# Row 0's first loads as float32 through SyncE, row 7's loads earlier, late stores in parts, and a new order of the work

## The chip, the cores and the metric

The kernel runs on one core of a Trainium2 chip. TensorE (PE) multiplies matrices into PSUM; VectorE (DVE), ScalarE (ACT) and GpSimd (POOL) do the elementwise work; SyncE (SP) issues transfers. Sixteen DMA engines move data between the chip's main memory and the on-chip SBUF. Each compute engine works through its own list of instructions in order and waits for others by semaphores. The metric is the device time of one execution in microseconds; the kernel before has a median of 102.69 us over three runs (101.49 to 103.97).

## The reference

Windowed attention is followed by a gated low-rank mixture of experts, with 8 batch rows, 8 heads, 576 positions and a head size of 64. Four heads see the last 32 positions, four see every fourth of the last 128. Everything is float32.

```python
scores = scale * np.matmul(q, k.transpose(0, 1, 3, 2))
scores = np.where(masks, scores, -1e9)
attn = np.exp(scores - scores.max(-1, keepdims=True))
x = np.matmul(attn / attn.sum(-1, keepdims=True), v)      # -> (4608, 512)
logits = x @ w_gate                                       # 8 experts
topk = np.argpartition(-logits, 2, axis=1)[:, :2]         # the two largest
w = softmax(logits at topk)
out = x + sum over the two experts of w * ((x @ A[e]) @ B[e])   # rank 16
```

## The kernel before, in words

The work is cut into 8 rows (`r`, one for each batch entry) and two head groups (`g`; 0 and 1). Each step is an operation with a name, and the name carries its row and group. For one row:

- **Loads.** `L...` on GpSimd's queue brings q, k and v and casts float32 to bfloat16 on the way, into one of four slots of SBUF. Row 0 has four of them (`Lk00`: q and k of group 0; `Lk01`; `Lv00`, `Lv01`: v), row 1 two (`L10` and `L11`), rows 2 to 6 one each, row 7 eight (`Lq7gh` with q and k, `Lv7gh` with v, for each group and each half of the partitions). A row from 4 on reuses a slot, and its load waits for the scores and values of the row four before.
- **Scores.** `S0rg` and `S1rg` (two parts of five and four segments) first multiply a mask into PSUM and then q and k on top; `E0rg` and `E1rg` on ScalarE take the exponential (line 341).
- **Values.** `Vrg` multiplies by v, which carries a column of ones for the sum; `Rrg` (line 377) takes the reciprocal and `Nrg` (line 380) divides, both on VectorE, into the float32 tile `x`. `Brg` (line 387) on GpSimd casts to bfloat16.
- **Adapters.** `Trg` and `Ur` transpose on TensorE (lines 404 and 428), `Crg`, `Cdr`, `Cpr` copy back on ScalarE; `Z0r` and `Z1r` multiply by the first weights, `Y..` copies; a chain of small VectorE steps finds the two largest logits; `gzr` (line 489, GpSimd) gates, `Gr` transposes, `gcr` and `gnr` copy; `Drn` multiplies by the second weights and `Arn` adds to `x`.
- **Store.** `Or` on SyncE's queue writes `x` out (lines 582 and 586): rows 0 to 5 whole, rows 6 and 7 in two halves by group. Each store waits for its row's sums and for a list `late` of row 7's loads: the four `Lq7..` and two of the `Lv7..`. Stores with a two-letter name also wait for the store before the last, so that at most two are under way.

Ahead of all this come constants (`con`, a SyncE load; `cc`, `cd` on ScalarE), the adapter weights (`awf` by ScalarE's queue, line 242, cast by `awc` on VectorE; `btf` by SyncE's queue, line 243, cast by `btc` on ScalarE), cleared tiles (`pz`, `xz`, `vz`), and scratch matmuls on a zero tile that keep TensorE occupied: `warm` (five) and `F0`, `F1`, `F2` (two, two, one), each one issued as two passes. All TensorE operations but transposes are issued through a helper at line 211.

What sets the order is a text, `PLAN`: a list of operation names, with the PSUM bank behind an `@`. Operations are issued in that order, each one to its engine's list, so each engine's order is that of the text. Loads stand in GpSimd's list between its casts and gates, stores in SyncE's. In the old text the first scratch matmuls stand ahead of row 0, `F0` behind its first scores, `F1` behind `V01`, and `F2` behind `T00`. Row 0's first scores wait for `Lk00`.

Of the kernel before, what the change touches and what calls it, by code (L numbers as in the profile page):

```python
# [6 lines left out]
FP = mybir.dt.float32  # L7
# [157 lines left out]
def program(nc=None, qkv=None, aw=None, bt=None, con=None, out=None):  # L165
# [10 lines left out]
    XB = [sb(f"xb{i}", [128, 2, XG], BF) for i in range(2)]  # L176
    XT = [sb(f"xt{i}", [128, 4, 640], BF) for i in range(2)]
# [46 lines left out]
    scratch("warm", 5, ["wz"], 1.05)  # L224
    for i, (_, n) in enumerate(FILL):
# [6 lines left out]
    add("cc0", "ACT", ("el", SEG), lambda: [nc.scalar.copy(CON[:, 0:SEG], ONE[:, 0:SEG])], ["con"])  # L232
    add("cc1", "ACT", ("el", 5 * SEG), lambda: [nc.scalar.copy(
        CON[:, 3 * SEG :].rearrange("p (s n) -> p s n", s=5), ONE[:, 0:SEG].unsqueeze(1).to_broadcast([128, 5, SEG]))], ["con"])
# [7 lines left out]
    add("awf", "ACT", ("dma", 128, 2176), lambda: [nc.scalar.dma_start(out=AWF[:, :], in_=aw)])  # L242
    add("btf", "SP", ("dma", 128, 2048), lambda: [nc.sync.dma_start(out=BTF[:, :], in_=bt)])
# [12 lines left out]
    for i in range(SLOTS):  # L256
        for a in range(2):
            if i < 2:
                add(f"vz{i}{a}", "DVE", ("zero", 1170), lambda i=i, a=a: [nc.vector.memset(zeros(i, a), 0)])
            else:  # L260
                add(f"vz{i}{a}", "ACT", ("el", 1170), lambda i=i, a=a: [nc.scalar.copy(
                    zeros(i, a).bitcast(FP), WARM[half(a), 0:2].bitcast(FP).to_broadcast([64, 1170]))], ["wz"])
# [17 lines left out]
    def loads(r):  # L280
        if r == 0:
            for g in range(2):
                a = load(f"Lk{r}{g}", r, [(h, QK_AT[h][g], QK) for h in range(2)], [])
                b = load(f"Lv{r}{g}", r, [(h, V_AT[h][g], VB) for h in range(2)], [])
                qk_ready[r, g], v_ready[r, g] = [a], [b]
# [18 lines left out]
    def attention(r, g):  # L304
        t = IN[r % SLOTS] if nc is not None else None
        i = (2 * r + g) % NP
# [4 lines left out]
        for part, (b0, nb) in enumerate(((0, 5), (5, 4))):  # L311
            k = Bank(2)

            def scores(b0=b0, nb=nb, k=k):
# [13 lines left out]
                for j in range(nb):  # L328
                    n = SEG if b0 + j < NB - 1 else 64
                    for pr, a, c in tiles:  # L330
                        q = QK_AT[a][g] + pr * S + 64 * (b0 + j)
                        done.append(mm(
                            PS[half(c), k.at + pr, j * SEG : j * SEG + n],
                            t[half(a), q + 2 * S : q + 2 * S + 64], t[half(a), q : q + n], False, j == nb - 1,
# [3 lines left out]
            s = add(f"S{part}{tag}", "PE", ("s", nb, 4 + 4 * nb), scores, qk_ready[r, g] + ["con"] + cuts * g, k)  # L338
# [20 lines left out]
        def values():  # L359
# [24 lines left out]
            [va, rc], k)  # L384
        cut = 512 if (r, g) == (B - 1, 1) else XG
        free = [f"T{r - 2}{g}", f"U{r - 2}"] if r > 1 else []
# [186 lines left out]
    for r in range(B):  # L573
# [4 lines left out]
        adapters(r)  # L578
    for r in range(B):
        more = [f"A{r}3"] if r in SHARED else []  # L580
        if r < B - 2:
            add(f"O{r}", "SP", ("dma", 128, 9216), lambda r=r: [nc.sync.dma_start(out=out[r], in_=X[r][:, :])],
                [f"A{r}{n}" for n in range(3)] + more + late)
        else:
            for g in range(2):
                add(f"O{r}{g}", "SP", ("dma", 128, 4608), lambda r=r, g=g: [nc.sync.dma_start(
                    out=out[r][:, XG * g : XG * g + XG], in_=X[r][:, XG * g : XG * g + XG])],
                    [f"A{r}{g}", f"A{r}2"] + more * (1 - g) + late)
# [12 lines left out]
Z01@7 Y01 S021@5 m01 top1 E021 S020@3 S120@1 s121 tt1 th1 g21 gz1 E020  # L601
V21@5 E120 G1@3 R21 gn1 V20@0 gc1 N21 D12@3 R20 D11@6 vz31 A12 N20
S030@4 B20 E030 D10@0 S130@2 E130 S131@4 E131 B21 A11 A10 S031@6 E031 L5
U2@0 T21@5 V30@1 Cd2 T20@4 R30 C21 N30 B30 V31@5 Cp2 R31 N31 L6
C20 Z12@0 Y12 Z02@1 Y02 m02 m12 s122 S141@2 E141 S140@5 E140 T30@7 S041@1
tt2 th2 E041 B31 U3@0 S040@5 C30 V41@1 Cd3 Cp3 top2 g22 gz2 G2@0
E040 gn2 gc2 R41 N41 T31@4 V40@5 D22@3 R40 A22 N40 C31 Z03@0 Z13@2
Y03 m03 Y13 S150@3 m13 s123 D20@0 E150 S151@6 E151 S051@4 D21@2 top3 tt3
th3 B41 B40 A20 T41@7 E051 g23 A21 gz3 U4@1 T40@0 C41 Lq700
Lq711 Lq701 S050@2 Lv710 Cp4 V51@5 R51 N51 Cd4 G3@1 E050 V50@2 R50 N50  # L610
C40 gn3 Z14@0 gc3 B51 Y14 Z04@5 Y04 S060@0 B50 D30@6 E060 S160@4 Lq710
E160 Lv711 Lv701 S161@2 E161 D32@1 Lv700 A30 T50@0 S061@6 A32 C50 m14 m04
top4 V60@1 s124 tt4 T51@4 th4 U5@0 E061 V61@5 O0 R60 N60 O1 S170@2
Cp5 g24 C51 Cd5 Z05@1 E170 R61 Z15@4 Y05 Y15 gz4 N61 G4@0 B60
gn4 D31@6 m05 gc4 B61 S070@2 E070 S171@4 A31 m15 T60@0 top5 E171 s125
tt5 th5 g25 S071@6 O2 O3 V70@1 R70 T61@4 E071 C60 V71@5 U6@0 N70
# [65 lines left out]
```

## Time and profile before

| what | before |
|---|---|
| median of three runs | 102.69 us (101.49 to 103.97) |
| span of the profiled execution | 99.7 us (its whole time isn't given apart from the span) |
| PE, ACT, DVE, POOL busy | 82%, 72%, 61%, 50% |
| casting loads on GpSimd's queue (q0) | 14.23 MB written, 71.2% of 16 engines |
| SyncE's transfers (q1) | 9.77 MB, 23.8% |
| read from and written to main memory | 29.07 MB and 9.44 MB, 386 GB/s over the span |

The span runs from the first to the last instruction of one profiled execution; the runs' times include what lies around it. Queue q0 counts the bytes as written in bfloat16; it reads twice as many. The page cuts the span in 40 slices, with the busy share of each in tenths, and ends with the chain of work that ended last. A stretch of a trace gives, in this order, its length, the busy time of PE, weight loads, DVE, ACT and POOL, the granted TensorE clock, the DMA share and GB/s. A line of the timeline gives start, duration, engine, source line, operation and, in brackets, how long the engine had stood idle and what released it.

### The profile page before, as it was taken

Reading aid. Unit: us, or ns where it says so; the run is one execution under the profiler, and the core shown is the slowest. Engines: PE = TensorE matmul, PEld = TensorE weight load, DVE = VectorE, ACT = ScalarE, POOL = GpSimd, SP = SyncE. Lnnn points to the kernel's source line nnn. Section 1 sums busy time; section 2 is a strip of 40 time slices with the busy share of each in tenths; the row PEclk is TensorE's granted clock in tenths of the full one; section 3 lists DMA queues with packets and bytes.
Section 4 is the critical chain, followed back from the end, with each engine's and each line's share of the span. In section 5 each row is a group of like instructions: output and inputs, shape, how many; then the busy total and the mean of one; then the engine's idle time right before and its main releaser. Section 6 shows DMA issues by size and latency. Waiting matters only on the chain.

```text
span 99.7 us, 3591 instructions
## 1 busy us (share of the span) xinstructions
PE 81.6 (82%) x1585; PEld 59.4 (60%) x1585; DVE 61.3 (61%) x138; ACT 71.7 (72%) x123; POOL 50.1 (50%) x68
## 2 busy tenths in 40 slices
PE   5994989997886879779988997999999999867300
PEld 3331476466653757458856875787788888745100
DVE  5800008854589237945954599197598499989700
ACT  5830771398798897598599588979979999956300
POOL 5999001860453050480872445848448328666810
PEclk9999999999999999999999999999999999999965
DMA  2999999998999989999898999897899999869994
GB/s 51 290 194 183 200 218 208 219 262 182 234 212 196 245 190 252 193 206 235 184 257 184 226 218 198 123 203 157 133 241 408 422 410 422 358 288 414 414 412 183
DMA packets 4447, 24.50 MB, mean 246 GB/s; under 512 B 720, under 2 KB 848, under 8 KB 3024
## 3 DMA queue, kind: packets, MB, share of 16 engines
q0 software_dynamic: 2560, 14.23, 71.2%
q1 hardware_dynamic: 1728, 9.77, 23.8%
q10 hardware_dynamic: 144, 0.28, 0.8%
q8 instruction: 12, 0.20, 0.7%
q14 instruction: 3, 0.02, 0.1%
HBM read 29.07 MB, written 9.44 MB: 386 GB/s over the span
## 4 chain that ended last, share of the span: by engine, by line
PE 53%; ACT 18%; DMA 8%; DVE 7%; POOL 6%; issue 4%; POOLq 0%
PE ps L211 46%; ACT p L341 8%; DMA in<-in_qkv_dram 8%; PE ps L404 4%; DVE x L380 3%; POOL gz L489 3%; PE ps L494 3%; ACT xt L414 2%; POOL x L549 1%; DVE x L541 1%; POOL xb L387 1%; ACT xt L417 1%; DVE tt L479 1%; ACT th L481 1%; ACT zs L462 1%
## 5 line engine op out<-in xcount | busy, mean ns | idle before, releaser
L341 ACT ACTIVATE p<-ps 128x960 bf16<-128x960 f32 (+1 forms) x32 | 27.6, 892 | 7.9 <-PE ps L211 7.6
L387 POOL CAST xb<-x 128x1152 bf16<-128x1152 f32 (+1 forms) x16 | 17.6, 1113 | 23.4 <-DVE x L380 23.4
L211 PE MATMUL ps<-in,p 128*64 128x130 bf16 (+1 forms) x416 | 21.4, 221 | 1.4 <-ACT p L341 1.0
L380 DVE TENSOR_TENSOR x<-ps,rec 128x1152 f32<-128x1152 f32 x16 | 21.7, 1356 | 0.5
L211 PEld LDWEIGHTS ps<-in,p 128*64 128x64 bf16 (+1 forms) x416 | 17.1, 104 | 4.6 <-ACT p L341 1.6
L377 DVE RECIPROCAL rec<-ps 128x18 f32<-128x18 f32 x16 | 4.3, 270 | 22.7 <-PE ps L211 22.5
L541 DVE TENSOR_TENSOR x<-x,ps 128x1024 f32<-128x1024 f32 (+1 forms) x16 | 17.3, 1113 | 1.2 <-PE ps L211 1.2
L271 POOL DMA_DIRECT2D in<-in_qkv_dram x32 | 16.9, 564 | 0.8 <-POOLq L665 0.8
L489 POOL TENSOR_TENSOR gz<-zs,g 128x640 bf16<-128x640 f32 x7 | 8.9, 1274 | 16.1 <-DVE g L484 16.1
L211 PE MATMUL ps<-warm 128*128 128x512 f32 x20 | 12.2, 751 | 1.2 <-DVE warm L215 1.2
L211 PE MATMUL ps<-aw,xt 128*128 128x136 bf16 x160 | 11.2, 223 | 1.0 <-ACT xt L420 0.4
L211 PEld LDWEIGHTS ps<-in 64*64 64x64 bf16 x576 | 10.7, 106 | 2.1
L211 PE MATMUL ps<-in 64*64 64x96 bf16 (+1 forms) x576 | 11.5, 200 | 0.0
L414 ACT COPY xt<-ps 128x1024 bf16<-128x1024 bf16 x8 | 8.1, 1016 | 4.1 <-PE ps L404 4.0
L211 PEld LDWEIGHTS ps<-aw,xt 128*128 128x128 bf16 x160 | 9.6, 98 | 1.9 <-ACT xt L420 0.7
L404 PE MATMUL ps<-one,xb 128*128 128x128 bf16 x128 | 9.6, 220 | 0.7 <-issue 0.5
L404 PEld LDWEIGHTS ps<-one,xb 128*128 128x128 bf16 x128 | 7.6, 97 | 2.2 <-POOL xb L387 0.9
L462 ACT COPY zs<-ps 128x408 f32<-128x408 f32 (+1 forms) x14 | 6.1, 443 | 3.4 <-PE ps L211 3.3
L211 PE MATMUL ps<-bt,gc 128*128 128x256 bf16 (+1 forms) x48 | 6.7, 256 | 1.5 <-ACT gc L510 0.7
L211 PEld LDWEIGHTS ps<-warm 128*128 128x128 f32 x20 | 4.4, 239 | 5.8 <-issue 4.5
L211 PE MATMUL ps<-bt,gn 128*128 128x256 bf16 (+1 forms) x48 | 6.9, 264 | 1.1 <-DVE x L380 0.5
L211 PE MATMUL ps<-one 64*64 64x384 bf16 (+1 forms) x64 | 5.9, 361 | 2.4 <-DMA in<-in_qkv_dram 1.8
(53 smaller groups left out, 91.9 us busy)
## 6 DMA issues: line engine op xcount, KB each, us to landing
in<-in_qkv_dram POOLq DMA_DIRECT2D x10, 868.5 KB, 17.7
out_dram<-x SPq DMA_DIRECT2D x6, 1152.0 KB, 5.8
in<-in_qkv_dram POOLq DMA_DIRECT2D x10, 288.0 KB, 6.8
out_dram<-x SPq DMA_DIRECT2D x4, 576.0 KB, 3.5
in<-in_qkv_dram POOLq DMA_DIRECT2D x10, 146.2 KB, 8.2
in<-in_qkv_dram POOLq DMA_DIRECT2D x2, 434.2 KB, 14.5
awf<-in_aw_dram ACTq DMA_DIRECT2D x1, 272.0 KB, 2.8
btf<-in_bt_dram SPq DMA_DIRECT2D x1, 256.0 KB, 3.1
```

The lines of the kernel that those rows point to most:

```text
L211: return nc.tensor.matmul(o, lhsT=lhsT, rhs=rhs, start=start, stop=stop, skip_group_check=True)
L271: nc.gpsimd.dma_start(out=IN[r % SLOTS][half(a), at : at + n], in_=qkv[r, a, :, at - 2 * VB * a : at - 2 * VB * a + n],)
L341: return [nc.scalar.activation(p[:, :, :].rearrange("p h (s c) -> p h s c", c=PER)[:, :, b0 : b0 + nb, 0:SEG], PS[:, k.at : k.at + 2, 0 : ...
L377: rc = add(f"R{tag}", "DVE", ("el", 60), lambda: [nc.vector.reciprocal(rec[:, :].rearrange("p (b i) -> p b i", b=3), PS[:, k.at : k.at + 3 ...
L380: nm = add(f"N{tag}", "DVE", ("el", XG), lambda: [nc.vector.tensor_tensor(X[r][:, XG * g : XG * g + XG].rearrange("p (b i n) -> p b i n", ...
L387: add(f"B{tag}", "POOL", ("el", cut), lambda: [nc.gpsimd.tensor_copy(XB[r % 2][:, g, 0:cut], X[r][:, XG * g : XG * g + cut])], [nm] + free)
L404: nc.tensor.transpose(tp[j][:, 128 * u : 128 * u + 128], xb[:, g, 256 * u + 128 * j : 256 * u + 128 * j + 128], ident())
L414: return [nc.scalar.copy(xt[:, 0:2, 0:S].rearrange("p j (c i) -> p j c i", c=C)[:, :, :, 0:128], tp.rearrange("p j (i c) -> p j c i", c=C))]
L462: zc.append(add(f"Y{st}{r}", "ACT", ("el", len(us) * ZW), lambda us=us, k=k: [nc.scalar.copy(zs[:, us[0] : us[-1] + 1].rearrange("p u n -> ...
L489: return [en.tensor_tensor(GZ[i][:, us[0] : us[0] + n, :].rearrange("p u (e r) -> p u e r", e=E), zv()[:, us[0] : us[0] + n, 0:ER].rearran ...
L494: return [nc.tensor.transpose(bank(k, n).bitcast(BF)[:, 128 * u : 128 * u + 128], GZ[i][:, u], ident()) for n in range(k.size) for u in us ...
L541: return [nc.vector.tensor_tensor(v, v, PS[:, k.at : k.at + nk].rearrange("p b n -> p (b n)"), ALU.add)]
```

## The change

Five things change together.

1. Row 0's q and k of group 0 no longer come by `Lk00`. SyncE fetches them as float32 into the tile of `x` that row 5 uses much later (`H0`, columns 0 to 351 of each of the four segments, and `H1`, 352 to 575; two transfers each). VectorE casts the q half, ScalarE the k half (`h00`, `h01`, `h10`, `h11`) into the `xb` tile of row 1 (`FIRST`), and row 0's first scores read them there. Scores of part 0 wait for the casts of `H0`; those of part 1 for all four. The cast of row 1 into that tile waits for these scores.
2. The weights `awf` and `btf` wait for `H1`. In the new text `awf` stands behind row 0's exponentials in ScalarE's list.
3. Row 7's loads stand elsewhere in the text: `Lq701` and `Lq700` behind row 2's transposes, `Lv711`, `Lq710` and `Lv701` around row 5's scores, the last three behind row 6's first steps. The list `late` has only `Lq700` and `Lq701`.
4. Rows 4 to 6 are stored in halves, row 7 in four parts, the last of them a quarter of the row's main part.
5. The order text is new throughout. Scratch matmuls `warm` are three instead of five, and all of `F0`, `F1`, `F2` stand ahead of row 0's first scores.

```diff
+    FIRST = XB[1][:, :, :].rearrange("p g n -> p (g n)") if nc is not None else None
...
-    scratch("warm", 5, ["wz"], 1.05)
+    scratch("warm", 3, ["wz"], 1.05)
...
-    add("awf", "ACT", ("dma", 128, 2176), lambda: [nc.scalar.dma_start(out=AWF[:, :], in_=aw)])
-    add("btf", "SP", ("dma", 128, 2048), lambda: [nc.sync.dma_start(out=BTF[:, :], in_=bt)])
+    early, parts = X[5], ((0, 352), (352, S))
+    for n, (c0, c1) in enumerate(parts):
+        def fetch(c0=c0, c1=c1):
+            return [nc.sync.dma_start(
+                out=early[half(a), :].rearrange("p (s n) -> p s n", s=4)[:, :, c0:c1],
+                in_=qkv[0, a, :, QK_AT[a][0] - 2 * VB * a : QK_AT[a][0] - 2 * VB * a + QK].rearrange("p (s n) -> p s n", s=4)[:, :, c0:c1],
+            ) for a in range(2)]
+
+        add(f"H{n}", "SP", ("dma", 128, 16 * (c1 - c0), 2), fetch)
+        for x, (eng, s0) in enumerate((("DVE", 0), ("ACT", 2))):
+            def cast(c0=c0, c1=c1, s0=s0, eng=eng):
+                o, i = [t[:, 576 * s0 : 576 * s0 + 1152].rearrange("p (s n) -> p s n", s=2)[:, :, c0:c1] for t in (FIRST, early)]
+                return [nc.vector.tensor_copy(o, i) if eng == "DVE" else nc.scalar.copy(o, i)]
+
+            add(f"h{n}{x}", eng, ("el", 2 * (c1 - c0)), cast, [f"H{n}"] + ["tab"] * x)
+    add("awf", "ACT", ("dma", 128, 2176), lambda: [nc.scalar.dma_start(out=AWF[:, :], in_=aw)], ["H1"])
+    add("btf", "SP", ("dma", 128, 2048), lambda: [nc.sync.dma_start(out=BTF[:, :], in_=bt)], ["H1"])
...
-                late.extend(qk_ready[r, g] + v_ready[r, g] * g)
+                late.extend(qk_ready[r, g] * (1 - g))
...
-                        q = QK_AT[a][g] + pr * S + 64 * (b0 + j)
+                        q = (0 if first else QK_AT[a][g]) + pr * S + 64 * (b0 + j)
+                        w = FIRST if first else t
...
+            ready = [f"h{n}{x}" for n in range(part + 1) for x in range(2)] if first else qk_ready[r, g]
...
+        free = [f"T{r - 2}{g}", f"U{r - 2}"] if r > 1 else ["S000", "S100"] if r == 1 else []
...
+        if r < 4:
+            store(f"O{r}", r, [(0, 2 * XG)], [f"A{r}{n}" for n in range(3)])
+        elif r < B - 1:
+            for g in range(2):
+                store(f"O{r}{g}", r, [(XG * g, XG * g + XG)], [f"A{r}{g}", f"A{r}2"] + more * (1 - g))
+        else:
+            store(f"O{r}0", r, [(0, 512)], [f"A{r}0"])
+            store(f"O{r}1", r, [(XG, XG + 1024)], [f"A{r}1"])
+            store(f"O{r}2", r, [(1024, XG), (XG + 1024, 2 * XG)], [f"A{r}2"])
+            store(f"O{r}3", r, [(512, 1024)], more)
...
-con awf btf wz tab cc0 pz1 pz0 Lk00 cc1 vz21 vz00 Lk01 xz0
-vz01 warm@7 cd3 Lv00 xz1 cd2 S100@1 pz3 cd0 Lv01 L11 S000@5 E000 F0@4
-btc cd1 L10 E100 S001@6 S101@4 V00@1 E101 awc L2 E001 V01@5 R00 F1@0
-N00 B00 T00@4 C00 R01 F2@3 N01 B01 U0@6 Cp0 Cd0 T01@7 C01
-L3 L4 S111@2 S011@0 Z00@7 E011 Y00 Z10@0 vz10 vz11 Y10 pz2 m00 m10
-s120 E111 S110@6 S010@4 top0 tt0 th0 g20 E110 gz0 E010 V11@0 R11 N11
-G0@7 V10@3 B11 R10 gc0 N10 gn0 D02@7 D00@0 B10 A02 T11@6 vz20 D01@2
-vz30 C11 U1@7 Cd1 Cp1 T10@4 A00 C10 S121@0 E121 A01 Z11@2 Y11 m11
...
+wz warm@3 F2@1 tab con cc1 cd3 pz2 F0@3 vz00 vz10 pz3 H0 H1
+F1@0 pz0 vz11 h10 Lv00 cd2 Lk01 Lv01 L11 L10 vz20 L2 h00 L3
+pz1 cc0 h11 h01 S100@0 vz31 cd1 cd0 E100 S000@3 E000 vz01 V00@2 R00
+N00 S001@0 S101@6 E101 E001 V01@3 R01 B00 N01 awf awc xz0 T00@6 C00
+S011@4 S111@0 E011 E111 B01 U0@3 T01@7 Cd0 V11@4 C01 L4 R11 Cp0 Z00@2
+btf Y00 Z10@3 N11 Y10 S010@4 E010 m10 S110@0 m00 s120 top0 B11 tt0
+th0 g20 gz0 E110 V10@3 G0@7 R10 vz21 xz1 T11@6 N10 btc B10 gc0
+D01@0 S121@3 gn0 C11 E121 A01 L5 S021@5 E021 S120@1 S020@3 T10@0 V21@5 R21
+N21 E020 E120 V20@1 R20 C10 U1@4 Cp1 D02@5 N20 Cd1 Z01@6 D00@2 vz30
...
```

More of the change, by code (lines that the diff above doesn't have):

```diff
@@ L305, in attention @@
         t = IN[r % SLOTS] if nc is not None else None
+        first = r == g == 0
         i = (2 * r + g) % NP
@@ L578, in program, with store, emit @@
         adapters(r)
+    def store(name, r, cuts, deps):
+        def emit():
+            return [nc.sync.dma_start(out=out[r][:, c0:c1], in_=X[r][:, c0:c1]) for c0, c1 in cuts]
+        add(name, "SP", ("dma", 128, 4 * sum(c1 - c0 for c0, c1 in cuts), len(cuts)), emit, deps + late)
     for r in range(B):
         more = [f"A{r}3"] if r in SHARED else []
-        if r < B - 2:
-            add(f"O{r}", "SP", ("dma", 128, 9216), lambda r=r: [nc.sync.dma_start(out=out[r], in_=X[r][:, :])],
-                [f"A{r}{n}" for n in range(3)] + more + late)
-        else:
[L585 to L588, printed above, removed]
+        if r < 4:
[3 more added lines that the diff above has]
+                store(f"O{r}{g}", r, [(XG * g, XG * g + XG)], [f"A{r}{g}", f"A{r}2"] + more * (1 - g))
+        else:
+            store(f"O{r}0", r, [(0, 512)], [f"A{r}0"])
+            store(f"O{r}1", r, [(XG, XG + 1024)], [f"A{r}1"])
+            store(f"O{r}2", r, [(1024, XG), (XG + 1024, 2 * XG)], [f"A{r}2"])
+            store(f"O{r}3", r, [(512, 1024)], more)
@@ L601 @@
[L601 to L616, printed above, removed]
```

48 lines of the change are left out of this document (31 added, 17 removed).

## The prediction

> **What bounds the kernel now.** I read the page first: its first two parts, the DMA queues, and the chain that ended last.
>
> ```profile
> span 99.7 us, 3591 instructions
> ...
> PE 81.6 (82%) x1585; PEld 59.4 (60%) x1585; DVE 61.3 (61%) x138; ACT 71.7 (72%) x123; POOL 50.1 (50%) x68
> ...
> DMA  2999999998999989999898999897899999869994
> ...
> q0 software_dynamic: 2560, 14.23, 71.2%
> q1 hardware_dynamic: 1728, 9.77, 23.8%
> ...
> PE 53%; ACT 18%; DMA 8%; DVE 7%; POOL 6%; issue 4%; POOLq 0%
> ```
>
> Two things run nearly without rest. TensorE is busy 82% of the span and is 53% of the chain. The 16 DMA engines stand at 9 in almost every slice; GpSimd's loads (q0) and SyncE's transfers (q1) together take 95% of them. The table of stretches says where the DMA does rest.
>
> ```profile
> 4.00:62.00 58.00, 49.84 (x1003) 34.86 (x1001) 32.69 (x71) 41.90 (x67) 26.10 (x35) 1.00 1.03 213
> ...
> 62.50:65.00 2.50, 2.50 (x69) 2.15 (x71) 0.56 (x2) 2.28 (x6) 1.88 (x4) 1.00 0.77 114
> 67.50:70.00 2.50, 2.50 (x86) 1.78 (x76) 1.92 (x8) 2.34 (x4) 2.30 (x4) 1.00 0.71 138
> 85.00:87.50 2.50, 2.10 (x30) 1.76 (x28) 2.46 (x13) 2.10 (x5) 1.51 (x2) 1.00 0.84 342
> 87.50:90.00 2.50, 1.66 (x23) 1.09 (x20) 2.20 (x12) 1.36 (x3) 1.46 (x2) 1.00 0.75 313
> 95.00:97.50 2.50, 0.00 (x0) 0.00 (x0) 0.00 (x0) 0.00 (x0) 0.00 (x1) 0.54 1.00 409
> ```
>
> The columns are the stretch, its length, busy time of PE, weight loads, DVE, ACT and POOL, the clock, the DMA share and GB/s. From 4 to 62 us the share is 1.03: no rest. The rests are (1-0.77) + (1-0.71) + (1-0.84) + (1-0.75) = 0.93 stretches of 2.5 us, 2.3 us in all: 1.3 us among row 7's loads and 1.0 us among the stores. From 95 us no engine works and the DMA still writes at 409 GB/s. So the end is the end of the DMA's work, and the DMA's work is the same bytes after the change. That caps what can be won; the tensor order decides whether the cap is reached.
>
> **The change, part by part.**
>
> *Row 0's first q and k through SyncE.* Their 1.18 MB of float32 (2 halves x 64 rows x 2304 x 4 bytes) leave the GpSimd queue and come first on SyncE's; the weights, 0.53 MB, come behind. First the DMA in the first 20 us, in slices of 0.5 us, then TensorE's weight loads up to its first scores:
>
> ```profile
> GB/s 0 0 0 24 238 357 381 342 184 175 184 194 175 230 184 157 184 203 212 172 182 210 187 206 201 237 231 198 212 231 175 205 224 233 200 227 222 195 222 222
> ```
>
> ```profile
> 6.46 0.20 PEld L211 LDWEIGHTS ps<-warm 128*128 128x128 f32 x1 [0.52 <-issue]
> 6.91 0.19 PEld L211 LDWEIGHTS ps<-warm 128*128 128x128 f32 x1 [0.24 <-issue]
> 7.34 0.19 PEld L211 LDWEIGHTS ps<-warm 128*128 128x128 f32 x1 [0.24 <-issue]
> 9.62 0.11 PEld L211 LDWEIGHTS ps<-one 64*64 64x64 bf16 x4 [2.10 <-DMA in<-in_qkv_dram]
> ```
>
> Between 2 and 4 us only SyncE's and ScalarE's float32 transfers move (238 to 381 GB/s); GpSimd's loads follow at about 184 GB/s counted in bfloat16. Today the weights use that early stretch; afterwards the float32 q and k do. So nothing is gained for the DMA, only another transfer is first. By 4 us some 0.66 MB have moved, 0.6 MB of it q and k; the other 0.6 MB share the engines with GpSimd's loads. Alone, at 360 GB/s, they would end at 5.7 us; at half the engines at 7.3 us; at a sixth (small runs of 1408 and 896 bytes taking turns with runs of 4.7 to 9.2 KB) at 14 us. I take 7.3 us and add 1 us for the last of 16 engines: 8.3 us.
>
> The casts, by the nearest rows:
>
> ```profile
> L245 ACT ACTIVATE bt<-btf 128x512 bf16<-128x512 f32 x1 | 0.6, 622 | 0.0
> ...
> L244 DVE CAST aw<-awf 128x544 bf16<-128x544 f32 x1 | 0.5, 529 | 0.0
> ```
>
> Each engine casts 448 and 704 elements: 1152/544 x 0.53 = 1.1 us on VectorE, 1152/512 x 0.62 = 1.4 us on ScalarE. The first scores of the new order are part 1, which needs all four casts, so 8.3 + 1.4 = 9.7 us. But TensorE is not free then. The new order runs all eight scratch matmuls ahead of the first scores, where five stand now. Each is two passes; the tenth starts at 7.34 us and passes by then are 0.43 us apart, so the sixteenth starts at 7.34 + 6 x 0.435 = 9.95 and ends at 10.4 us. **The first scores start at 10.4 us instead of 9.62**, whatever the early transfer does up to a landing at 9.0 us.
>
> By the Trainium skill, "DMA: Bandwidth & Descriptors", section "Queues, rings and completion order", an engine goes round the queues it has work for and drains a whole packet of about 9 to 17 descriptors before it switches. By that rule SyncE's small runs go 16 at a time and the 7.3 us is right, perhaps late; if single descriptors took turns it would be 14 us. No row here shows which: in this trace the two queues hardly overlap.
>
> *What a later or earlier start is worth.* TensorE is held by loads again later:
>
> ```profile
> 21.56 1.56 PE L211 MATMUL ps<-aw,xt 128*128 128x136 bf16 x20 [0.24 <-ACT xt L417]
> 23.65 0.36 PE L211 MATMUL ps<-one 64*64 64x384 bf16 x4 [0.53 <-DMA in<-in_qkv_dram]
> ...
> 27.89 0.25 PE L211 MATMUL ps<-bt,gn 128*64 128x128 bf16 x2
> ...
> 27.97 0.22 PE L211 MATMUL ps<-bt,gc 128*64 128x128 bf16 x2
> ...
> 28.12 0.61 PE L211 MATMUL ps<-bt,gn 128*128 128x256 bf16 x4
> ...
> 30.85 0.28 PE L428 MATMUL ps<-one,xb 128*128 128x128 bf16 x2 [0.60 <-POOL xb L387]
> 30.98 0.61 PE L404 MATMUL ps<-one,xb 128*128 128x128 bf16 x8
> ...
> 31.89 0.36 PE L211 MATMUL ps<-con,one 64*64 64x384 bf16 x4 [0.30 <-DMA in<-in_qkv_dram]
> ```
>
> Row 1's second load is awaited at 23.65, row 2's at 31.89. The bytes ahead of row 2 are the same in both kernels, weights included, so that gate stays at about 31.9 us. What differs is how much of rows 0 and 1 is done by then. In the old order D02, D00, U1 and T10 (0.25 + 0.22 + 0.61 + 0.28 + 0.61 = 2.0 us, the rows from 27.89 to 30.98) stand ahead of row 2's first scores; in the new one they stand behind. TensorE reaches the gate with 2.0 us more left to do. Against that, TensorE idles 58 - 49.84 = 8.2 us between 4 and 62 us, most of it waiting for such gates, and work in hand fills part of those. Bounds: the whole 2.0 us later, or 1.5 us sooner if the new order fills nearly all idle time. I take 0.7 us later.
>
> *Weights behind.* Their cover is the time until the first product with them, now at 21.56. By rows already shown the new order gets there at about 23.4 us. ScalarE's queue issues the first weights after the four exponentials of row 0, at about 17 us: first scores at 10.4, two pairs of scores and of exponentials with one value product between. VectorE's cast of them stands ahead of row 1's reciprocals, and TensorE has row 1's second scores behind that product.
>
> ```profile
> awf<-in_aw_dram ACTq DMA_DIRECT2D x1, 272.0 KB, 2.8
> btf<-in_bt_dram SPq DMA_DIRECT2D x1, 256.0 KB, 3.1
> ...
> in<-in_qkv_dram POOLq DMA_DIRECT2D x10, 288.0 KB, 6.8
> in<-in_qkv_dram POOLq DMA_DIRECT2D x10, 146.2 KB, 8.2
> ```
>
> At 2.8 us they land at 19.8 and cost nothing; at the 8.2 us of loads of a like size among others they land at 25.2, are cast at 25.7, and TensorE, VectorE and all behind them are 2.3 us late. I take nothing, being nearest to the row of the same transfer.
>
> *Small runs.* The early transfer moves in runs of 1408 and 896 bytes. At the 342 to 381 GB/s of the 2 KB runs it takes 3.3 us of the DMA; as casting load it took 0.59 MB / 213 GB/s = 2.8 us. I take 0.5 us more DMA time, with bounds of 0 and 1.5.
>
> *Row 7's loads and the stores.*
>
> ```profile
> 62.26 2.12 POOL L271 DMA_DIRECT2D in<-in_qkv_dram  x4
> ...
> 68.79 2.05 POOL L271 DMA_DIRECT2D in<-in_qkv_dram  x4
> ```
>
> ```profile
> 73.53 15.82 SPq L582 DMA_DIRECT2D out_dram<-x  x6
> 91.49 3.87 SPq L586 DMA_DIRECT2D out_dram<-x  x4
> ```
>
> The eight pieces are issued in two clumps, and each store waits for six of them. In the new order two pieces go out behind row 2's transposes, three more around row 5's scores, and the stores wait for the first two alone. That removes the 1.3 us of rest around 62 and 69 us, and with 0.86 MB fewer to wait for (4 us at 213 GB/s) stores begin some 5 us sooner. Only sooner, though: row 7's three last pieces then share the engines with them. Of the 1.0 us of rest at 85 to 90 us, where the DMA waits for rows 4 and 5 to be ready, halved stores recover perhaps half; a tensor order that is 0.7 us late gives that back. Each of the late rows' stores costs another issue on SyncE, which has nothing else to do.
>
> *The last store.*
>
> ```profile
> 93.74 1.26 POOL L549 TENSOR_TENSOR x<-x,btf 128x512 f32<-128x512 f32 x1 [0.24 <-ACT btf L547]
> ```
>
> The last sum ends at 95.0, and 4.7 us pass to the end of the span: a store of 576 KB behind others. A last store of 256 KB would take some 3 us (the 3.1 us of the weights of that size). It counts only if the queue ahead of it is empty, which the 409 GB/s from 95 to 97.5 deny. I take 0.2 us.
>
> *Sum.* DMA rests removed -1.3; store rests 0; small runs +0.5; order +0.7, of which the DMA's slack at the end hides 0.4, so +0.3; last store -0.2. Together -0.7 us: a span of 99.0. The page gives the span alone; the median of the runs, 102.69, lies 3.0 above it, and I keep that: **102.0 us**.
>
> **Rivals.**
>
> *Faster: the order fills the gaps.* The DMA never rests from 2 us to the end and TensorE keeps ahead of the stores: -2.3 for the rests, -0.5 for the last store, +0.4 for small runs: 100.3 us. For it speaks that 8.2 us of TensorE's idle time lie open; against it that TensorE reaches row 2 with more left, and that the stores of rows 5 to 7, 3.5 MB or 8.6 us at 409 GB/s, are not all ready while the DMA still rests in the stretch from 87.5 us. 0.15.
>
> *Slower: SyncE's and ScalarE's transfers are starved by the loads.* If small runs take turns one by one with GpSimd's large ones, q and k land at 14 us instead of 8.3 and the scores start at 15.4, 5 us after the scratch matmuls; the first weights, too, come 2.3 us late. The point from which it decides is a landing after 9.0 us, or of the weights after 22.8. TensorE, VectorE and ScalarE all stand behind. Some 2 us are made up in idle time, so +3 on the forecast: 105.0 us. 0.2.
>
> *Row 7's last pieces come late.* They are issued in the midst of stores of 9 KB runs; row 7's last scores and values wait 1 to 2 us and the tail with them: 103.3 us. 0.12.
>
> *Forecast*, 0.53: the change doesn't do what it sets out to do at the start (the scores do not come sooner), and gains a little at the end.
>
> **How the numbers follow.** About 2% is what a measurement of this kernel can tell from no change: its three runs lie 2.4% apart. The forecast's own range is 101.2 to 103.0. With the fast case at 100.3 and the starved one at 105.0, from which half is kept, the range is 100.0 to 104.8. Faster by over 2% (below 100.6) is nearly all of the fast case: 0.15. Slower by over 2% (above 104.7) is most of the starved case and a remainder of the others: 0.2. The rest, 0.65, is within 2%.
>
> **What would show it.** Right: first scores at about 10.4 us, preceded directly by scratch matmuls with no DMA wait; row 2's first scores again near 32 us with a wait for a load; the DMA share near 1.0 at 62 to 70 us; stores from about 68 us. Wrong: a wait for VectorE or ScalarE ahead of the first scores well past 10.4 us; a wait for the weights' cast at row 0's first product with them; loads of row 2 that land before 30 us; or a DMA that ends well before 97 us, since then it is not the bound I took it for.

## The result, and the profile after

The changed kernel takes 122.15 us in the median of four runs (121.8 to 124.18); the kernel before, on the same chip, 102.36 (101.49 to 103.97). The ratio is 1.195, with a 95% interval of 1.187 to 1.203. The prediction was 102.0 with a range to 104.8: its starved rival had the mechanism, and a price of 3 us for transfers that cost 14 to 19 of the 20. Runs of one kernel lie up to some 5% apart, so where a reading hangs on it the lowest run stands beside the median.

The page of the changed kernel, in the order in which the prediction read the old one: busy tenths, clock and DMA in 40 slices of 3 us, then the chain that ended last.

```profile
span 120.3 us, 3598 instructions
...
PE   6993000575688074898898994999999969997510
...
PEclk9999955557755959999999999999999999999995
DMA  2999999998998997049999995696899453094995
...
PE 34%; DMA 25%; ACT 18%; DVE 14%; issue 3%; SPq 2%; POOL 2%; POOLq 0%
```

TensorE does nothing from the fifth slice to the seventh, its clock then stands at half, and transfers are 25% of the chain instead of 8%. The DMA row has holes where there were none. How large they are says the table of stretches (stretch, length, PE, weight loads, DVE, ACT, POOL, clock, DMA share, GB/s), whole spans first:

```profile
0.00:99.70 99.70, 81.60 (x1585) 59.41 (x1585) 61.27 (x138) 71.70 (x123) 50.05 (x68) 0.98 0.97 246
```

```profile
0.00:120.30 120.30, 83.72 (x1581) 63.23 (x1581) 61.07 (x140) 72.10 (x125) 49.15 (x66) 0.89 0.82 209
...
10.00:20.00 10.00, 0.00 (x0) 0.00 (x0) 0.00 (x0) 0.00 (x0) 0.00 (x0) 0.74 1.08 228
20.00:27.50 7.50, 4.36 (x82) 3.32 (x86) 2.55 (x6) 4.49 (x7) 0.00 (x0) 0.50 1.03 225
...
47.50:52.50 5.00, 4.02 (x107) 3.21 (x107) 2.83 (x3) 4.90 (x8) 2.88 (x4) 1.00 0.05 9
...
72.50:77.50 5.00, 3.27 (x61) 3.03 (x62) 2.50 (x4) 2.07 (x4) 2.41 (x2) 1.00 0.54 164
...
95.00:105.00 10.00, 9.06 (x176) 7.70 (x175) 6.84 (x16) 9.01 (x19) 5.78 (x6) 1.00 0.31 124
```

Share times span is the DMA's work: 0.97 x 99.7 = 96.7 us before, 0.82 x 120.3 = 98.6 after. The shares are rounded; summed packet by packet in the traces the work is 96.5 and 99.2. It grew by 2 to 3 us, and the rests, the difference to the span, grew from about 3 to about 21. So the DMA's work is nearly the same, and some 18 of the 20.6 us are rests of the DMA. They lie late (47.5 to 52.5, 72.5 to 77.5, 95 to 105 us), but their cause lies early. The timeline of the changed kernel shows it (start, duration, engine, line, operation, in brackets the idle time before and what ended it):

```profile
20.17 1.25 ACT L255 CAST xb<-x 128x448 bf16<-128x448 f32 x2 [15.20 <-DMA x<-in_qkv_dram]
...
21.56 0.53 PE L212 MATMUL ps<-one 64*64 64x384 bf16 x4 [11.58 <-ACT xb L255]
...
24.77 2.28 PE L212 MATMUL ps<-in,p 128*64 128x130 bf16 x26 [1.58 <-ACT p L359]
...
28.72 0.37 ACTq L258 DMA_DIRECT2D awf<-in_aw_dram  x1
...
42.13 0.44 DVE L260 CAST aw<-awf 128x544 bf16<-128x544 f32 x1 [8.65 <-DMA awf<-in_aw_dram]
...
42.72 2.43 PE L212 MATMUL ps<-aw,xt 128*128 128x136 bf16 x20 [3.98 <-DVE aw L260]
```

The early q and k are cast from 20.17 us, not 8.3. The first scores start at 21.56 instead of 9.62, after 11.58 us in which TensorE waited for them. Then the weights, issued at 28.72, are cast at 42.13: 13.4 us for a transfer that took 2.8 us before; the first product with them starts at 42.72 instead of 21.56. How lateness at the start becomes rest of the DMA shows in GpSimd's list, where row 5's load waits for row 1 to give up its slot and stands behind a cast of row 1:

```profile
43.48 1.10 POOL L271 DMA_DIRECT2D in<-in_qkv_dram  x2
```

```profile
34.63 1.03 POOL L287 DMA_DIRECT2D in<-in_qkv_dram  x2
...
52.03 1.10 POOL L287 DMA_DIRECT2D in<-in_qkv_dram  x2
```

Before (the first fence), row 5's load is issued at 43.48 us. In the changed kernel (the second), row 4's goes out at 34.63, has landed by 47.5, and row 5's follows at 52.03: between them the DMA has no load to do and a share of 0.05.

### The profile page after: what moved, and what is told of

It reads as the page before. It is cut to its first block, busy times and chain, and to the rows that moved or that the text cites. A ratio compares the mean times of both kernels' runs of the same rounds, so it can differ in the third digit from the quotient of the medians.

```text
span 120.3 us, 3598 instructions
## 1 busy us (share of the span) xinstructions
PE 83.7 (70%) x1581; PEld 63.2 (53%) x1581; DVE 61.1 (51%) x140; ACT 72.1 (60%) x125; POOL 49.1 (41%) x66
## 4 chain that ended last, share of the span: by engine, by line
PE 34%; DMA 25%; ACT 18%; DVE 14%; issue 3%; SPq 2%; POOL 2%; POOLq 0%
PE ps L212 30%; DMA x<-in_qkv_dram 14%; DMA awf<-in_aw_dram 11%; ACT p L359 7%; DVE x L398 6%; DVE x L559 5%; PE ps L422 2%; ACT in L277 2%; SPq L246 2%; PE ps L512 2%; ACT xt L435 2%; ACT gc L528 1%; ACT gn L531 1%; DVE rec L395 1%; POOL x L567 1%
## 5 line engine op out<-in xcount | busy, mean ns | idle before, releaser
L359 ACT ACTIVATE p<-ps 128x768 bf16<-128x768 f32 (+1 forms) x32 | 27.3, 892 | 7.8 <-PE ps L212 7.6
L212 PE MATMUL ps<-in,p 128*64 128x130 bf16 (+1 forms) x416 | 23.3, 233 | 7.5 <-ACT p L359 5.3
L212 PEld LDWEIGHTS ps<-in,p 128*64 128x64 bf16 (+1 forms) x416 | 18.7, 111 | 11.4 <-ACT p L359 6.5
L212 PE MATMUL ps<-aw,xt 128*128 128x136 bf16 x160 | 12.6, 235 | 4.3 <-DVE aw L260 4.0
L212 PEld LDWEIGHTS ps<-aw,xt 128*128 128x128 bf16 x160 | 10.8, 104 | 5.2 <-issue 4.2
L212 PE MATMUL ps<-in 64*64 64x96 bf16 x540 | 11.7, 210 | 0.0
L255 ACT CAST xb<-x 128x448 bf16<-128x448 f32 (+1 forms) x2 | 1.2, 670 | 15.2 <-DMA x<-in_qkv_dram 15.2
L212 PE MATMUL ps<-warm 128*128 128x512 f32 x16 | 8.8, 709 | 1.2 <-DVE warm L216 1.2
L212 PEld LDWEIGHTS ps<-one 64*64 64x64 bf16 x64 | 2.0, 110 | 13.7 <-DVE p L263 12.4
L212 PE MATMUL ps<-con,one 64*64 64x480 bf16 (+1 forms) x64 | 7.1, 407 | 2.7 <-DVE x L398 1.3
```

Source lines behind the costliest of these rows:

```text
L212: return nc.tensor.matmul(o, lhsT=lhsT, rhs=rhs, start=start, stop=stop, skip_group_check=True)
L359: return [nc.scalar.activation(p[:, :, :].rearrange("p h (s c) -> p h s c", c=PER)[:, :, b0 : b0 + nb, 0:SEG], PS[:, k.at : k.at + 2, 0 : ...
```

## The experiments

### Who gets the DMA engines: the early q and k

The view of the transfers, from 10 to 20 us of the changed kernel, has the two queues in packets, megabytes and share of the 16 engines:

```profile
DMA packets 1118, 2.28 MB, mean 228 GB/s; under 512 B 161, under 2 KB 640, under 8 KB 1118
## 3 DMA queue, kind: packets, MB, share of 16 engines
q0 software_dynamic: 601, 1.85, 92.6%
q1 hardware_dynamic: 517, 0.43, 15.9%
```

SyncE's queue (q1) moved 517 packets of 0.8 KB in the time in which GpSimd's (q0) moved 601 of 3 KB: about one for one. Some of them are 4 bytes long; without these it is 479 runs against 478. An engine thus gets 479/16 = 30 of SyncE's runs through in 10 us, and the early q and k are 1024 runs (2 halves x 64 rows x 4 segments x 2 parts), 64 for each engine. The counts alone would also fit turns of many runs each, if both queues had equally many in a turn. The start times of the single packets in the trace decide it: in these 10 us a packet of GpSimd's queue starts within 6 ns of the end of each of the 479 small runs. The Trainium skill, "DMA: Bandwidth & Descriptors", section "Queues, rings and completion order", has an engine drain a packet of about 9 to 17 descriptors from one queue before it goes on to the next; the trace disagrees, with a change of queue after every one of these 479 runs. Four kernels vary who takes turns with whom.

**GpSimd's loads wait for the early transfer.**

```diff
-  v_ready[r, g] = [load(f"Lv{r}{g}", r, ..., [])]
+  v_ready[r, g] = [load(f"Lv{r}{g}", r, ..., [] if g else ["H1"])]
```

> The changed kernel, but GpSimd's first loads wait until the early q and k have landed, so that these are alone on the DMA engines. Theory (turns): an engine takes the runs of the two queues in turn, one by one, so the small early runs are slow only beside GpSimd's long ones; alone the early q and k land by 6.5 us (after: 20.15), and the first scores start when the scratch matmuls end, about 9.5 us. Rival (making the runs): 1024 small runs are slow to make whoever else is there; they land after 12 us here too. Time: the DMA loses about 3 us at the start, the weights still land late; 110 to 116 us by the theory, 120 or more by the rival.

113.11 us (one run). The page's transfers up to 10 us (GB/s in steps of 0.25 us; size, us from issue to landing), then TensorE's first scores:

```profile
GB/s 0 0 0 0 0 0 0 164 98 0 39 39 101 253 372 377 220 237 225 242 270 206 227 200 225 233 269 215 247 215 211 83 11 0 0 0 0 0 0 25
...
x<-in_qkv_dram SPq DMA_DIRECT2D x2, 352.0 KB, 4.7
x<-in_qkv_dram SPq DMA_DIRECT2D x2, 224.0 KB, 5.5
```

```profile
10.87 0.36 PE L212 MATMUL ps<-one 64*64 64x384 bf16 x4
```

Alone, the transfer ends at about 8 us and is cast at 8.85, later than the 6.5 expected and well before the rival's 12; the scores follow the scratch matmuls at 10.87, as the prediction had it at 10.4. But even alone the small runs settle at 200 to 270 GB/s, not the 360 that the prediction took. The loads are now issued 8 us late (9.12 instead of 1.23 us) and the weights still take 9.3 us; the kernel stays 11% slower than before.

**Whole runs.** Each partition's q and k in one run of 9216 bytes, 8 for each engine in place of 64.

```diff
-    early, parts = X[5], ((0, 352), (352, S))
+    early, parts = X[5], ((0, S),)
-  out=early[half(a), :].rearrange("p (s n) -> p s n", s=4)[:, :, c0:c1]
+  out=early[half(a), 0:QK]
...
```

> The changed kernel, but the early q and k come in whole runs of 9216 bytes, 8 for each DMA engine instead of 64, beside GpSimd's loads as in the change. Theory (turns): landing by 7.5 us, first scores at about 9.5 us; the weights, still behind row 0's exponentials and 8 runs for each engine, take about 9 us beside runs of 1.04 us and land near 28 us, 4 to 5 us after they are needed; 105 to 110 us in all. Rival (a share by bytes: a queue of 1.18 MB gets its share whatever the runs): landing still after 12 us, 115 us or more. Rival (the new order itself is slow): 112 us or more, with first scores at 9.5 us.

116.0 us median (113.27 to 119.38, four runs).

```profile
x<-in_qkv_dram SPq DMA_DIRECT2D x2, 576.0 KB, 7.9
```

```profile
12.57 0.36 PE L212 MATMUL ps<-one 64*64 64x384 bf16 x4 [1.22 <-ACT xb L255]
```

The same bytes in an eighth of the runs land 9 us earlier, at 11.27. Part of that is a head start: GpSimd's loads begin to move at 4.4 us here, at 2.6 in the changed kernel, and 46 of the 128 runs had gone by then. A share by bytes would not give 9 us; the number of turns counts. But the theory's price was wrong: it had the landing at 7.5 and the time at 105 to 110 us, and the lowest run took 113.27. A run of 9216 bytes takes 0.56 to 0.75 us itself in this trace, and the weights took 11.1 us.

**Weights first, small runs behind them.**

```diff
-    add("awf", "ACT", ..., ["H1"])
-    add("btf", "SP", ..., ["H1"])
+    add("awf", "ACT", ...)
+    add("btf", "SP", ...)
-wz warm@3 F2@1 tab con cc1 ... pz3 H0 H1
+con awf btf wz warm@3 F2@1 tab cc1 ... pz3 H0 H1
...
```

> The changed kernel with the weights first again, the early q and k in small runs as changed. Theory (turns): early q and k land at 20 us or a little later, first scores at 21.5 to 23 us, but no wait for the weights' cast at 38 to 43 us; 115 to 119 us, so that the late weights are worth 4 to 6 us of the 19. Rival (the weights' lateness costs nothing more once everything is late): 121 us or more.

133.16 us median (130.61 to 134.01): far slower than the change itself, and outside the theory's range.

```profile
36.48 0.53 PE L212 MATMUL ps<-one 64*64 64x384 bf16 x4 [26.05 <-ACT xb L255]
```

```profile
q0 software_dynamic: 696, 2.63, 92.2%
q1 hardware_dynamic: 690, 0.69, 17.0%
```

I had missed what the weights' early place would do: they take the stretch before GpSimd's loads, in which part of the small runs had gone alone. In the changed kernel only 210 of the 504 small runs from 4 to 10 us are followed at once by a packet of GpSimd's. The second fence is 10 to 24 us: 690 packets against 696, one for one, and each of the 647 small runs among them is followed by a packet of GpSimd's; the transfers are cast at 35 us.

**Two queues.** The half with `a = 1` goes by ScalarE's queue, both issued first.

```diff
-            return [nc.sync.dma_start(
+            return [(nc.sync, nc.scalar)[a].dma_start(
...
-wz warm@3 F2@1 tab con cc1 ... pz3 H0 H1
+con H0 H1 wz warm@3 F2@1 tab cc1 ... pz3
```

> The changed kernel with one half of the early q and k on SyncE's queue and the other half on ScalarE's, both issued first; the runs and their bytes are the same. Theory (each DMA engine gives the queues turns, run by run): two queues give the small runs two turns where they had one, so q and k land at 11 to 13 us instead of 20.2, first scores at 12.5 to 14.5 us, 114 to 118 us in all. Rival (the small runs are slow by themselves, or the engines share by bytes): landing at 18 us or later, 120 to 123 us.

114.42 us median (113.79 to 118.19); ratio to before 1.121 (1.114 to 1.129). From 6 to 12 us, and the first scores:

```profile
q0 software_dynamic: 333, 0.93, 78.0%
q1 hardware_dynamic: 313, 0.27, 17.8%
q10 hardware_dynamic: 266, 0.22, 13.5%
```

```profile
13.97 0.53 PE L212 MATMUL ps<-one 64*64 64x384 bf16 x4 [2.86 <-ACT xb L255]
```

Three queues take turns, about one run each, and q and k are cast at 12.58 us instead of 20.17. Landing, scores and time fall into the ranges of the theory. Part of it may come from the issue, whose last part is 1.3 us earlier, and from a head start: 204 of the 1024 runs had gone when GpSimd's loads began to move, at 3.7 us. The weights took 15.3 us here; the profile is that of the run of 118.19 us.

### What each transfer costs

**The first two parts alone, in the old order.** Early q and k, weights behind; old loads of row 7, old stores.

```diff
-con awf btf wz tab cc0 pz1 pz0 Lk00 cc1 ...
+con H0 H1 wz tab cc0 pz1 pz0 cc1 ...
-... E001 V01@5 ...
+... E101 awf btf awc L2 E001 btc V01@5 ...
```

> The kernel before with the first two parts of the change alone: row 0's first q and k in small float32 runs through SyncE, cast on two engines, and the weights behind; old order of the engines, old loads of row 7, old stores. Theory (SyncE's and ScalarE's runs take turns one by one with GpSimd's): q and k land at 19 to 22 us, first scores at 21 to 23 us, weights 9 to 14 us after their issue, 113 to 119 us. Rival (only together with the new order, which puts all behind the early transfer, is it this slow): 108 us or less.

121.58 us median (120.65 to 124.73, six runs), ratio 1.188 (1.179 to 1.196). First scores at 22.21 us, inside the theory's range; the first weights needed only 4.0 us, for they were issued as GpSimd's loads paused (DMA share 0.45 from 29 to 33 us), and the time is above the range all the same. Their lateness counts even so: their cast stands ahead of row 0's reciprocals in VectorE's list, and VectorE waited for it for 11.07 us, until 33.03. In the old order these two parts alone cost 19%, nearly as much as the whole change. The DMA's work here is 0.83 x 118.9 = 98.7 us, and its rest 20.2.

**No early transfer, weights first; all else as changed.**

```diff
-    early, parts = X[5], ((0, 352), (352, S))   ... H0 H1, casts
-    add("awf", "ACT", ..., ["H1"])
+    add("awf", "ACT", ...)
-  qk_ready[r, g] = [load(f"Lk{r}{g}", ...)] if g else []
+  qk_ready[r, g] = [load(f"Lk{r}{g}", ...)]
-wz warm@3 F2@1 tab con cc1 ... pz3 H0 H1
+con awf btf wz warm@3 F2@1 tab cc1 ... pz3
...
```

> The changed kernel without the early q and k and with the weights first, as before the change: new order, scratch matmuls ahead, row 7's loads early, stores in parts. Theory (turns): all of the loss is in the two moved transfers, so 101 to 104 us, first scores at about 10 us. Rival (the new order itself is slow): 108 us or more.

107.82 us median (106.19 to 109.6; before in the same batch 102.3), between theory and rival and nearer the rival.

```profile
11.01 0.36 PE L212 MATMUL ps<-one 64*64 64x384 bf16 x4
...
24.32 1.36 PE L212 MATMUL ps<-aw,xt 128*128 128x136 bf16 x20
```

So 14 of the 20 us go with the two moved transfers, and 4 to 5 stay.

**The same with the weights behind.**

```diff
-con awf btf wz warm@3 ...
+con wz warm@3 ...
-... B00 N01 awc ...
+... B00 N01 awf awc ...
-    add("btf", "SP", ...)
+    add("btf", "SP", ..., ["E101"])
```

> The new order without the early transfer (107.8 us), its weights issued where the changed kernel issues them: the first behind row 0's exponentials, at 17 to 18 us, the second then too. Theory (starved twice: the weights by themselves also cost several us): they land 9 to 14 us after their issue, at 27 to 31 us, TensorE waits for their cast, and 111 to 114 us. Rival (only the early q and k cost anything, the weights' lateness lies beside other waits): 109 us or less.

113.19 us median (110.04 to 114.74), ratio 1.119 (1.109 to 1.129).

```profile
awf<-in_aw_dram ACTq DMA_DIRECT2D x1, 272.0 KB, 10.6
```

```profile
25.65 2.42 PE L212 MATMUL ps<-aw,xt 128*128 128x136 bf16 x20 [2.48 <-DVE aw L245]
```

The weights alone, issued at 14.5 us, cost 5.4 us by the medians (113.2 against 107.8, in two batches) and 3.9 by the lowest runs (110.04 against 106.19). Counted from the first scores, the product with them starts 2.6 us later (15.9 us after them instead of 13.3) and takes 2.42 us instead of 1.36, at a granted clock of 0.50: 3.6 us together. The early q and k add the remaining 9 up to 122.2 (12 by the lowest runs). Both are starved in the same way: in the changed kernel the 128 runs of the first weights move from 32.29 to 40.49 us beside 120 runs of GpSimd's, each 1.04 us long.

**A bridge of scratch matmuls.** Twelve more of them in the idle stretch.

```diff
-FILL = (("S000", 2), ("V01", 2), ("S111", 1),)
+FILL = (("S000", 2), ("V01", 14), ("S111", 1),)
```

> The changed kernel with 12 more scratch matmuls ahead of the first scores, in the stretch in which TensorE is idle. The granted clock after the idle stretch was 0.50 and 26 products with the weights took 2.28 us instead of 1.34. Theory (the low clock after the idle stretch lies on the path): the clock stays at 0.9 or more from 10 to 27 us, and 118 to 120 us instead of 122. Rival (the loads, late anyway, set the pace): the clock is up, the time 121.5 to 123 us.

124.96 us median (121.83 to 126.85). The 26 products of 2.28 us that the expectation names are value products. The profile is that of a run of 125.86 us.

```profile
PEclk9999999999996555699999996579999999999985
```

```profile
42.32 2.42 PE L212 MATMUL ps<-aw,xt 128*128 128x136 bf16 x20 [6.46 <-DVE aw L260]
```

The clock stays up until the weights are awaited, and the product with them starts at 42.32 instead of 42.72: nothing is won, for the wait behind it is a transfer's. So the low clock at the first scores and values, where the bridge removes it, is not what the idle time costs. As the weights are awaited the clock falls again, and the product takes 2.42 us with the bridge as without; what the low clock costs there this kernel doesn't test. The lowest run, 121.83, is the changed kernel's lowest, 121.8; why the other three are slower stays open.

### The other parts: row 7, the stores, the order

**The third part alone** (row 7's loads early, stores waiting for two of them, late stores in parts), old order.

```diff
-                late.extend(qk_ready[r, g] + v_ready[r, g] * g)
+                late.extend(qk_ready[r, g] * (1 - g))
...
-... Cp2 R31 N31 L6
+... Cp2 R31 N31 L6 Lq701 Lq700
```

> The kernel before with the third part of the change alone: row 7's first two q-and-k loads right behind row 6's, the stores waiting for these two, the late rows' stores in halves and quarters; the engines' order is otherwise the old one, and the weights and row 0's q and k move as before. Theory (the new order of the engines costs the 5% that stand without the early transfer): 100 to 103 us, at or below the kernel before, with the DMA's rest between 62 and 70 us smaller. Rival (row 7's pieces among the stores cost it): 105 us or more, and row 7's scores wait for their loads.

104.76 us median (102.94 to 106.44); ratio 1.013 (1.005 to 1.020), between theory and rival, and too small to be sure of. The rest from 60 to 70 us goes (share 1.02 there, 0.89 before), but TensorE stands still twice as stores and loads run together, for nothing that the views show:

```profile
73.88 0.56 PE L404 MATMUL ps<-one,xb 128*128 128x128 bf16 x7 [2.04 <-issue]
...
79.86 0.21 PE L211 MATMUL ps<-in 64*64 64x64 bf16 x1 [0.70 <-issue]
```

The stores are not the only suspect. In the traces of this case TensorE stands still for over 0.55 us with nothing shown to wait for 27 times, and 26 of these stalls begin within 1.9 us after the start of a 16 KB packet of the instruction queue (q8), of which there is one in some 7 us; several come before any store, the longest of these, 2.44 us, at 36 us. The kernel before has twelve such packets too, and no such stall. That TensorE waits for its instructions there is likely and not shown.

The DMA then rests from 80 to 90 us (share 0.47): it is ahead of TensorE, and what it gained is given back.

**The stores' parts alone**, and **row 7's two loads alone**, each in the kernel before.

```diff
+            store(f"O{r}0", r, [(0, 512)], [f"A{r}0"])   ... halves and quarters; late as before
```

> The kernel before with the late rows' stores in halves and quarters alone: row 7's loads are where they were, and the stores wait for all that they waited for. Theory (the 1.3% that the third part costs in the old order comes from stores that start among row 7's loads, beside which TensorE stood still for 2.0 and 0.7 us): 101.5 to 102.5 us, no such stall. Rival (more and smaller stores cost it): 103.3 to 104 us.

```diff
-... R31 N31 L6
+... R31 N31 L6 Lq701 Lq700
-... C41 Lq700 Lq711 Lq701 S050@2 ...
+... C41 Lq711 Lv711 Lv701 S050@2 ...
```

> The kernel before with row 7's first two q-and-k loads right behind row 6's, and nothing else of the change: the stores wait for what they waited for. Theory (it removes part of the DMA's rest between 62 and 70 us, and no store shares the engines with a load): 101 to 102 us, at or just below the kernel before. Rival (the end is set by TensorE's last rows, so DMA time won there is worth nothing): 102 to 103 us.

102.66 us (100.93 to 104.43), ratio 1.001 (0.996 to 1.007), and 102.09 us (101.67 to 102.83), ratio 1.003 (0.999 to 1.007): no difference either way. The second kernel also moves two pieces of v forward, into the place that the two loads leave. If the 1.3% is real (the intervals overlap a little), what it needs is the combination with the shorter list `late`, which lets stores start among row 7's loads. That TensorE's two stalls are the way in which it costs is not shown: in the first of these kernels one of 1.77 us occurs at 53 us, before any store, and the time is that of the kernel before.

**New order without the early transfer, every store behind all of row 7's loads.**

```diff
-                late.extend(qk_ready[r, g] * (1 - g))
+                late.extend(qk_ready[r, g] + v_ready[r, g])
-... O0 ... O1 ... Lq711 E061 O2 ... Lv710 Z05@0
+... Lq711 E061 ... Lv710 O0 O1 O2 Z05@0
```

> The new order without the early transfer (107.8 us), with every store behind all eight loads of row 7. Theory (the order of the engines costs the 5%, not the stores among row 7's loads): 106 to 109 us. Rival (stores that share the engines with row 7's last pieces make them late): 104 us or less, and row 7's last pieces land sooner after their issue.

106.05 us median (105.32 to 107.46), ratio 1.036 (1.030 to 1.043). Row 7's loads issued after 60 us land 4.0 to 4.3 us after their issue instead of 4.5 to 10.7, and by the medians 1.8 us of 5.5 go (0.9 by the lowest runs, in two batches); most of the loss stays with the order.

**Half of each order**, changed at row 3's normalization (`N31`), first new and then old, and the reverse; loads and stores of the third part in both.

```diff
-PLAN = the new order
+PLAN = the new order up to N31, the rest in the old order
```

> No early transfer. The new order up to row 3's normalization (some 42 us), then the old order with the third part's loads and stores. Old order with that third part: 1.3% above the kernel before; new order: 5.3%. Theory (the new order loses in the first rows, where TensorE waits for exponentials and for free banks): 106.5 to 108 us. Rival (it loses in the last rows): 103 to 104.5 us.

108.71 us median (106.05 to 110.4).

```diff
-PLAN = the new order
+PLAN = the old order up to N31, the rest in the new order
```

> No early transfer. The old order up to row 3's normalization, then the new order. Theory (the new order loses in the first rows): 103 to 104.5 us. Rival (it loses in the last rows): 106.5 to 108 us. Both halves near 105: the loss is spread over the rows.

107.49 us median (105.88 to 108.95). By their medians both are in or above the range of a half that holds the loss (the lowest runs, 106.05 and 105.88, lie just below it), and neither beats 104.76. The halves don't add up; that a seam between two orders costs something of its own would explain it and is not shown. Which operations make the new order slow stays open. What its waits show, without the early transfer (waited for: us in all, times, longest; up to 60 us, kernel with no early transfer first, then the one before):

```profile
PE ps L212 <- ACT p L344: 5.4, 4, 1.9
PE ps L212 <- DVE x L383: 4.7, 6, 1.8
```

```profile
PE ps L211 <- DMA in<-in_qkv_dram: 2.1, 3, 1.3
...
PE ps L211 <- ACT p L341: 1.0, 3, 0.4
PE ps L211 <- DVE x L380: 0.7, 2, 0.5
```

The new order puts value products right behind their exponentials and scores right behind the normalization: 10.1 us of waits where the old one has 1.7, besides its 2.1 for loads. Not all of the loss need come from these: without the early transfer TensorE also has two of the unexplained stalls, 1.79 us up to 75.26 and 1.24 up to 81.93.

None of the kernels beats the one before.

## Why the prediction was wrong

**The bound.** That the DMA's work is the same and its end the end of the kernel held: 96.7 and 98.6 us of work. The conclusion drawn from it did not. It was used as a cap on gains; it is as well an account in which every rest is a loss.

**The landing of q and k: "I take 7.3 us and add 1 us".** This step failed. Measured 20.2 us, above even the highest bound of 14. Two terms were wrong. The runs take turns one by one, which the prediction named as a possibility and set aside; the sixth of the engines that it then gave them is what the trace has (15.9%). Its reason for half the engines doesn't hold either: if both queues drained equal packets of many runs, the small runs would have the same sixth. And the head start is missing: of SyncE's 1.25 MB up to 21 us 0.69 move from 4 to 10 us and 0.43 from 10 to 20, so 0.13 MB, constants among them, had moved by 4 us and not 0.6. Four issues of 0.6 to 0.7 us each stand ahead of the transfer (the last at 3.2 us), and alone its runs move at 200 to 270 GB/s for the most part, not at 360.

**The weights: "At 2.8 us they land at 19.8 and cost nothing".** Failed. 13.4 us from issue to landing in the changed kernel, 10.6 with the scores on time, 9.3, 11.1 and 15.3 in three more; the bound of 8.2 was too low as well. The row taken, that of the same transfer, was from the only stretch in which no load runs: the nearest row was the one of the same conditions, not of the same bytes. By themselves they cost 4 to 5 us.

**The rival's price: "Some 2 us are made up in idle time, so +3".** This is the step that made a wrong case out of a seen one. Its deciding point, a landing after 9.0 us, was right; both its conditions came true. What it had wrong is the size of the delays, 5 us at the scores and 2.3 at the weights. Beside the kernel with the new order and neither transfer moved, the first scores are 21.56 - 11.01 = 10.6 us late, and the first product with the weights 42.72 - 24.32 = 18.4, for the weights are issued behind the late exponentials and are starved as well. The time is 14.3 us longer (15.9 between the two profiled runs), so 2.5 to 4 us are made up, not much more than the prediction's 2. The rest comes back because rows follow each other through four slots: lateness at the start delays row 5's load, and the DMA rests.

**The casts and scratch matmuls.** Near: the casts take 1.25 us on ScalarE and 0.83 on VectorE (predicted 1.4 and 1.1), and with an early transfer the scores start at 10.87 us behind the scratch matmuls (predicted 10.4).

**The order: "I take 0.7 us later", at row 2's gate.** Under-sized. Without the early transfer row 2's first scores start at 32.02, as predicted, but they wait for VectorE and not for a load. The new order loses some 4 us beyond the third part's 1.3; TensorE's waits up to 60 us lie all along the rows, not at the four steps that stood in front of row 2, but which of them cost the time is not shown.

**Row 7 and the stores: -1.3 and 0.** In the old order the rest at 60 to 70 us went, as said. It was worth nothing, since the DMA that is ahead of TensorE rests later (0.47 from 80 to 90 us). The rival "row 7's last pieces come late" gave 103.3, and 1.3% on 102.69 is 104.0; but TensorE waits for no such load there.

**Small runs: +0.5 us.** The DMA's work is 2 to 3 us more, beyond the bound of 1.5.

## What to carry to other kernels

A transfer in small runs that shares the DMA engines with a stream of large ones is priced in turns: its runs per engine times the length of one of the other's. Alone on the engines, in few long runs or over two queues the same bytes had landed by 8.85, 11.27 and 12.58 us instead of 20.17, though none of these made the kernel as fast as before. And in a kernel whose rows go through a fixed number of slots, idle time makes up little of a lateness at the start (here 2.5 to 4 of 18.4 us): the rest comes back as rest of the very resource that bounds it.

## What I had not expected of the hardware

- The queues take turns run by run: 517 against 601 packets, 690 against 696, and 333, 313 and 266 with three queues; in the first two cases every one of 479 and 647 small runs is followed by a packet of the other queue.
- Alone on the engines, runs of 1408 bytes (4 to 5.5 us) and runs of 896 bytes (6 to 7.5 us) both move at 228 to 242 GB/s in steps of half a microsecond; from 3.5 to 4 us the former moved at 375.
- With TensorE idle from 9.98 us, the granted clock falls to 0.50 at 14.75 us, and 26 value products take 2.28 us instead of 1.34. The Trainium skill, "TensorE: Matmul & The Clock Gate", section "Part 1: The HAM clock gate", has half rate follow on an idle window of about 3.4 us; the trace agrees in kind, with 4.8 us. A clock kept up until the first scores won nothing here.
- TensorE stands still for up to 2.74 us with nothing shown to wait for, in 26 of 27 cases just after the start of a 16 KB packet of the instruction queue; 2.04 us of it as stores run among casting loads.
